# A dense DFT convolution and hand-made gelu replaced by a two-step FFT, row layernorms and one-instruction gelu

## The chip, the core and the metric

One core of a Trainium2 chip. The metric is the time of one execution on the device in microseconds (us), as a median over runs. Before: 714.38 us (713.78 to 715.79, 12 runs).

The engines are called PE (TensorE, matmul), PEld (its weight load, which overlaps PE), DVE (VectorE), ACT (ScalarE), POOL (GpSimd) and SP (SyncE, which issues most DMAs). PSUM is the memory that matmuls write, SBUF the main on-chip memory. Every engine carries out its own instructions in the order in which the built program has them, and waits for the others by semaphores. `L284` is line 284 of the kernel concerned.

## The reference, cut to what matters

`q`, `k`, `v` are [1, 2048, 512] in bf16, S = 2048, D = 512, F = 1792.

```python
def ln(x): return (x - mean(x)) / sqrt(var(x) + 1e-5)          # over the 512 channels
k_shift = sum(shift_k[:, 3 - t] * k_pad[:, t:t + S] for t in range(4))   # causal, 4 taps
kv = k_shift * v
y  = irfft(rfft(kv, 4096) * rfft(ssm_k, 4096))[:S] + kv * ssm_D        # along the sequence
h  = q + ln(q) * y
x  = ln(h)
g  = gelu(ln(x) @ w1)                                           # tanh form of gelu
hs = shift_four_channel_quarters(g, +1, -1, +2, -2) @ w2
x1 = x + hs
out = h + x1 + gelu(ln(x1) @ w3) @ w4
```

## The kernel before

It works channel by channel: a tile is [128 channels, 2048 positions], four of them. The long convolution is a dense Fourier transform by matmul. For each chunk of 128 frequencies, DVE and ACT generate a cosine and a sine table, and PE multiplies them into `kv` and the filter `hf`, 4 x 16 matmuls of 512 columns:

```python
for b in range(NB):                       # 16 blocks of 128 positions; 16 chunks around this loop
    nc.tensor.matmul(ghr[:], lhsT=lhs_c, rhs=hf[:, b, :], start=st, stop=sp)        # L258
    nc.tensor.matmul(akr[:], lhsT=lhs_c, rhs=kv_all[:, b, :], start=st, stop=sp)
    nc.tensor.matmul(ghi[:], lhsT=lhs_s, rhs=hf[:, b, :], start=st, stop=sp)
    nc.tensor.matmul(aki[:], lhsT=lhs_s, rhs=kv_all[:, b, :], start=st, stop=sp)
# ... copies to SBUF, complex product; then the inverse, 512 matmuls in the same manner (L319, L321)
```

Since a layernorm then runs across partitions, its sums are matmuls with a column of ones, and mean and scale are spread to all partitions by matmuls with diagonal matrices (`layernorm_feat`, L121 to L178). Gelu is six instructions, two on ACT and four on DVE:

```python
def gelu_psum(gp, psrc, dst):
    nc.scalar.copy(xs[:], psrc)
    nc.vector.tensor_tensor(out=u[:], in0=xs[:], in1=xs[:], op=MUL)
    nc.vector.tensor_scalar(out=u[:], in0=u[:], scalar1=GELU_C2, scalar2=GELU_C1, op0=MUL, op1=ADD)
    nc.vector.tensor_tensor(out=u[:], in0=u[:], in1=xs[:], op=MUL)
    nc.scalar.activation(sg[:], u[:], ACT.Sigmoid)
    nc.vector.tensor_tensor(out=dst, in0=xs[:], in1=sg[:], op=MUL)
```

## Time and profile before

| stage before | us | length | the busiest |
|---|---|---|---|
| loads, kv, layernorm of q, dense DFT and inverse | 0 to 460 | 460 | PE from 100 on |
| layernorm of h, w1, w2, layernorm of x1 | 460 to 577 | 117 | DVE |
| w3, gelu, w4, output | 577 to 713 | 136 | PE, held back by the gelu relay |

The first cut lies at the end of the inverse's last matmul, the second at the first MLP matmul. The lines of the profile behind this table are shown in the prediction. A window line there gives, for a stretch of time, what each engine was busy; a group line gives a kind of instruction with its count, total busy time, mean duration in ns, and the idle time of the engine before it with what ended it. The granted clock is the share of its full rate that PE was given.

### The profile page before, as it was taken

How to read it: one execution, taken by the hardware profiler on the slowest of the kernel's cores; microseconds unless marked ns; L12 is line 12 of the kernel's file. 1: busy time of each engine (PE TensorE's matmuls, PEld its weight loads, DVE VectorE, ACT ScalarE, POOL GpSimd, SP SyncE). 2: the span in 40 equal slices, each digit the busy share in tenths (PEclk: the TensorE clock that was granted, in tenths of full speed). 3: DMA queues.
4: the chain of work that ended last, by engine and by line, in shares of the span. 5: the costliest groups of instructions: out<-in, count | busy, mean ns of one | idle time of the engine just before them, and what ended most of it. 6: DMA issues, size and time to landing. Idle time of an engine off the chain costs nothing.

```text
span 712.8 us, 7378 instructions
## 1 busy us (share of the span) xinstructions
PE 544.7 (76%) x2800; PEld 244.9 (34%) x2800; DVE 526.8 (74%) x1000; ACT 339.2 (48%) x391; POOL 2.9 (0%) x11
## 2 busy tenths in 40 slices
PE   0122459999999999995799999833558468999976
PEld 0011324444444444442344444331223323433422
DVE  4699693756756766616989997179887788888974
ACT  0323317466466456512978787112470256445460
POOL 1000000000000000000000000000000000000000
PEclk9999999999999999998799999955699579999997
DMA  5646000000000000000000000080000000000000
GB/s 118 132 101 120 1 1 0 1 1 0 1 1 0 1 1 0 1 1 0 0 1 1 0 1 1 0 266 0 1 0 0 2 0 1 30 1 29 1 30 30
DMA packets 39925, 15.68 MB, mean 22 GB/s; under 512 B 34513, under 2 KB 39378, under 8 KB 39890
## 3 DMA queue, kind: packets, MB, share of 16 engines
q1 hardware_dynamic: 29234, 10.76, 6.2%
q10 hardware_dynamic: 10656, 4.46, 2.4%
q8 instruction: 22, 0.36, 0.2%
q14 instruction: 13, 0.11, 0.0%
HBM read 4.72 MB, written 2.10 MB: 10 GB/s over the span
## 4 chain that ended last, share of the span: by engine, by line
PE 57%; DVE 24%; ACT 11%; DMA 4%; issue 3%; SPq 0%; ACTq 0%; DVEq 0%
PE yps L319 8%; PE yps L321 8%; PE ghr L258 8%; PE ghi L260 8%; PE akr L259 8%; PE aki L261 8%; ACT xs L336 4%; DVE u L338 3%; PE po L412 3%; ACT sg L343 3%; DMA vT<-in_A_v_dram 2%; DVE tn L177 2%; DVE g_sb L344 2%; DVE u L339 2%; DVE ksh L210 2%
## 5 line engine op out<-in xcount | busy, mean ns | idle before, releaser
L319 PE MATMUL yps<-ics,Qr 128*128 128x512 bf16 x256 | 98.4, 384 | 12.1 <-ACT ics L113 12.1
L112 ACT ACTIVATE e<-t 128x2048 f32<-128x2048 f32 (+2 forms) x34 | 63.1, 1856 | 80.3 <-DVE t L110 79.9
L321 PE MATMUL yps<-iss,Qi 128*128 128x512 bf16 x256 | 98.3, 384 | 0.0
L258 PE MATMUL ghr<-hf,cs 128*128 128x512 bf16 x240 | 91.0, 379 | 0.0
L259 PE MATMUL akr<-kv_all,cs 128*128 128x512 bf16 x240 | 91.0, 379 | 0.0
L260 PE MATMUL ghi<-hf,ss 128*128 128x512 bf16 x240 | 91.0, 379 | 0.0
L261 PE MATMUL aki<-kv_all,ss 128*128 128x512 bf16 x240 | 91.0, 379 | 0.0
L107 DVE TENSOR_TENSOR e<-bj,rv 128x2048 f32<-128x2048 f32 (+2 forms) x34 | 75.7, 2226 | 16.7 <-ACT cs L113 11.8
L110 DVE TENSOR_TENSOR t<-e,t 128x2048 f32<-128x2048 f32 (+2 forms) x34 | 75.8, 2228 | 1.0
L412 PE MATMUL po<-g_sb,w_sb 128*128 128x512 bf16 x224 | 64.0, 392 | 10.5 <-DVE g_sb L344 6.8
L217 PE MATMUL pt<-ident,kvTc 128*128 128x128 bf16 x64 | 14.0, 274 | 61.7 <-DVE kvTc L214 29.2
L272 DVE TENSOR_TENSOR p<-acr,gcr 128x512 bf16<-128x512 bf16 x16 | 6.8, 426 | 71.4 <-ACT acr L266 56.4
L405 PE MATMUL pg<-ln1T,w_sb 128*128 128x512 bf16 x224 | 56.7, 385 | 3.6 <-ACT bbc L173 1.2
L343 ACT ACTIVATE sg<-u 128x512 bf16<-128x512 bf16 x72 | 45.3, 631 | 24.6 <-DVE u L341 23.0
L166 PE MATMUL psbc<-dga,ones_pp 128*128 128x128 bf16 x64 | 17.2, 269 | 44.8 <-DVE dga L163 44.8
L336 ACT CAST xs<-pg 128x512 bf16<-128x512 f32 x56 | 32.7, 584 | 36.0 <-DVE g_sb L344 21.0
L108 DVE TENSOR_SCALAR t<-e 128x2048 f32<-128x2048 f32 (+2 forms) x34 | 40.6, 1194 | 1.9
L113 ACT ACTIVATE ics<-e,halfpi 128x2048 bf16<-128x2048 f32 x16 | 32.1, 2004 | 20.8 <-PE yps L319 20.7
L338 DVE TENSOR_TENSOR u<-xs 128x512 bf16<-128x512 bf16 x72 | 30.5, 423 | 13.4 <-ACT xs L336 12.6
L321 PEld LDWEIGHTS <-Qi 128*128 128x128 bf16 x256 | 25.3, 99 | 42.4 <-DVE t L110 11.9
L319 PEld LDWEIGHTS <-Qr 128*128 128x128 bf16 x256 | 25.3, 99 | 32.6 <-issue 3.5
L412 PEld LDWEIGHTS <-w_sb 128*128 128x128 bf16 x224 | 21.3, 100 | 40.9 <-issue 24.8
(124 smaller groups left out, 838.3 us busy)
## 6 DMA issues: line engine op xcount, KB each, us to landing
out_dram<-osb SPq DMA_DIRECT2D x16, 128.0 KB, 1.8
w_sb<-in_B_w_dram SPq DMA_DIRECT2D x1, 1792.0 KB, 8.8
w_sb<-in_B_w_dram ACTq DMA_DIRECT2D x1, 1792.0 KB, 14.8
w_sb<-in_B_w_dram SPq DMA_DIRECT2D x1, 512.0 KB, 12.0
w_sb<-in_B_w_dram ACTq DMA_DIRECT2D x1, 512.0 KB, 15.8
hf<-in_A_ssm_k_dram SPq DMA_TRANSPOSE x16, 2.6
vT<-in_A_v_dram ACTq DMA_TRANSPOSE x4, 4.2
kT<-in_A_k_dram SPq DMA_TRANSPOSE x4, 4.1
```

The lines of the kernel that those rows point to most:

```text
L107: nc.vector.tensor_tensor(out=ev, in0=bj_b, in1=rv_b, op=MUL)
L110: nc.vector.tensor_tensor(out=tv, in0=ev, in1=tv, op=SUB)
L112: nc.scalar.activation(ev, tv, ACT.Abs)
L258: nc.tensor.matmul(ghr[:], lhsT=lhs_c, rhs=hf[:, b, :], start=st, stop=sp)
L259: nc.tensor.matmul(akr[:], lhsT=lhs_c, rhs=kv_all[:, b, :], start=st, stop=sp)
L260: nc.tensor.matmul(ghi[:], lhsT=lhs_s, rhs=hf[:, b, :], start=st, stop=sp)
L261: nc.tensor.matmul(aki[:], lhsT=lhs_s, rhs=kv_all[:, b, :], start=st, stop=sp)
L319: nc.tensor.matmul(yps[:, c, :], lhsT=Qr[:, q, c * P:(c + 1) * P], rhs=ics[:, qi, :], start=(q == 0), stop=False)
L321: nc.tensor.matmul(yps[:, c, :], lhsT=Qi[:, q, c * P:(c + 1) * P], rhs=iss[:, qi, :], start=False, stop=False)
L336: nc.scalar.copy(xs[:], psrc)
L343: nc.scalar.activation(sg[:], u[:], ACT.Sigmoid)
L412: nc.tensor.matmul(po[:], lhsT=w4_sb[:, k2, m * P:(m + 1) * P], rhs=g_sb[:, k2, :], start=(k2 == 0), stop=(k2 == FC - 1))
```

## The change

The intent is to take the arithmetic of the convolution from a dense DFT of about 1600 wide matmuls to some 250, by splitting 4096 points into 64 x 64; to keep positions on the partitions ("row layout"), where a layernorm is a DVE statistic over 512 neighbours; and to let ACT do gelu in one instruction straight out of PSUM. The price is an exchange of data between the two steps of the transform, which goes through scratch memory in DRAM: `zh_d`, `zk_d` and `v_d`, each 4.2 MB written and read back. The core of a diff that is 833 lines long:

```diff
-# dense: 16 chunks x 4 x 16 forward matmuls, 512 inverse ones, tables made for each chunk
+def step1(x, zd, b, zc):                      # first 64-point step, one block of rows
+    ps = ps_s.tile([P, 2, D], F32, name="ps1", tag="ps1")
+    for t in range(2):
+        nc.tensor.matmul(ps[:, t, :], lhsT=f1[:, t, :], rhs=x, start=True, stop=True)
+    evac(zc[:, :, b % 2, :], ps[:])           # copy to SBUF, ACT and DVE in turn ("AV")
+    if b % 2 == 1:
+        nc.sync.dma_start(zd[:].rearrange(...)[:, :, b - 1:b + 1, :], zc)    # to DRAM
... (shift filter: 16 matmuls of 128 columns a block with diagonal matrices, then)
+    nc.vector.tensor_tensor(out=xkv[:, b, :], in0=pk[:], in1=v_sb[:, b, :], op=MUL)
... (zh, zk read back transposed; per frequency k1 of 32, the second step)
+    nc.tensor.matmul(a[:], lhsT=la, rhs=zk[:, k1, :], start=True, stop=True)         # psa L284
+    nc.tensor.matmul(g[:, 0, :], lhsT=lr, rhs=zh[:, k1, :], start=True, stop=True)   # psg
+    nc.tensor.matmul(g[:, 1, :], lhsT=li, rhs=zh[:, k1, :], start=True, stop=True)
+    nc.scalar.copy(asb[:], a[:])
+    nc.vector.tensor_tensor(out=pr[:], in0=g[:], in1=asb[:]..., op=MUL)              # pr L290
... (two psv matmuls, a copy vst, a store to v_d; wv read back; then per block)
-layernorm_feat(...)                           # sums and broadcasts on PE
+nc.vector.bn_stats(st[:, i, :], h_sb[:, b, :])
+nc.vector.bn_aggr(mv[:, i, :], st[:, i, :])
+rstd(r1[:], mv[:, :, 1], 1.0, 1e-5)           # Newton root: 9 small DVE instructions
+nc.vector.tensor_scalar(out=hb[:], in0=h_sb[:, b, :], scalar1=mv[:, i, 0:1], scalar2=r2[:, i:i + 1],
+                        op0=SUB, op1=MUL)
-gelu_psum(gp2, pg[:], g_sb[:, k2, :])         # six instructions
+nc.scalar.activation(gs[:, f, :], pg[:], ACT.Gelu_apprx_tanh)
... (loads, tables, halo, output per block: cut)
```

## The prediction

> **What bounds the kernel now.** I read the page's engine totals first, then the windows cut at the places where the chain of waits changes engine, then the groups for durations. The page:
>
> ```profile
> span 712.8 us, 7378 instructions
> PE 544.7 (76%) x2800; PEld 244.9 (34%) x2800; DVE 526.8 (74%) x1000; ACT 339.2 (48%) x391; POOL 2.9 (0%) x11
> PE 57%; DVE 24%; ACT 11%; DMA 4%; issue 3%; SPq 0%; ACTq 0%; DVEq 0%
> ```
>
> The last line is the chain that ended last: TensorE (PE) carries over half of it, VectorE (DVE) a quarter. An average over five stages says little, so the windows (start:end, length, busy us of each engine with its count, granted clock, DMA share, GB/s):
>
> ```profile
> 0.00:100.00 100.00, 23.34 (x224) 13.13 (x225) 77.89 (x132) 29.39 (x52) 2.75 (x9) 1.00 0.41 84
> 100.00:334.00 234.00, 230.50 (x1056) 103.39 (x1056) 139.16 (x185) 117.54 (x115) 0.00 (x0) 1.00 0.00 1
> 334.00:460.00 126.00, 117.06 (x528) 51.39 (x527) 103.96 (x73) 90.39 (x48) 0.00 (x0) 0.95 0.00 1
> 460.00:577.00 117.00, 56.53 (x481) 29.45 (x482) 96.04 (x288) 36.46 (x64) 0.15 (x2) 0.70 0.12 41
> 577.00:712.80 135.80, 117.25 (x512) 47.54 (x510) 109.75 (x327) 65.46 (x113) 0.00 (x0) 0.95 0.05 16
> ```
>
> Five stages: loads, kv and one layernorm (100 us, DVE the busiest); the dense forward DFT (234 us, PE busy without a gap); the dense inverse DFT (126 us, PE again); layernorms, w1 and w2 (117 us, DVE 82% busy, PE half idle and its clock at 0.70); the MLP (136 us, PE paced by the hand-made gelu). The bound is therefore PE for 360 us and DVE, or the DVE-ACT relay, for the rest. The groups and the order of time give the unit costs:
>
> ```profile
> L258 PE MATMUL ghr<-hf,cs 128*128 128x512 bf16 x240 | 91.0, 379 | 0.0
> L405 PE MATMUL pg<-ln1T,w_sb 128*128 128x512 bf16 x224 | 56.7, 385 | 3.6 <-ACT bbc L173 1.2
> L415 DVE TENSOR_TENSOR tf<-po,x1T 128x512 f32<-128x512 f32 x16 | 10.7, 688 | 1.4 <-PE po L412 1.1
> L177 DVE TENSOR_TENSOR tn<-xT,abc 128x512 bf16<-128x512 bf16 x16 | 6.1, 420 | 1.4 <-ACT abc L172 1.4
> L268 ACT CAST gcr<-ghr 128x512 bf16<-128x512 f32 x16 | 9.3, 583 | 19.6 <-PE ghr L258 18.5
> L343 ACT ACTIVATE sg<-u 128x512 bf16<-128x512 bf16 x72 | 45.3, 631 | 24.6 <-DVE u L341 23.0
> ...
> 118.93 0.38 PE L258 MATMUL ghr<-hf,cs 128*128 128x512 bf16 x1
> 119.15 0.38 PE L259 MATMUL akr<-kv_all,cs 128*128 128x512 bf16 x1
> 119.36 0.38 PE L260 MATMUL ghi<-hf,ss 128*128 128x512 bf16 x1
> 119.30 0.60 ACT L268 CAST gcr<-ghr 128x512 bf16<-128x512 f32 x1
> 119.78 0.61 ACT L269 CAST gci<-ghi 128x512 bf16<-128x512 f32 x1
> ```
>
> What to see: a 512-wide matmul lasts 379 ns but the next starts 0.216 us after it, so its price is 0.216. An ACT copy of 512 lasts 0.60 and costs 0.48. DVE neighbours overlap too: in the chain of waits two L328 products reading PSUM (matmul memory) take 1.29 us and two bf16 L177 products 0.67, so 0.60 to 0.64 and 0.34 each. I sum with these start-to-start prices.
>
> **What the Trainium skill says.** (1) "TensorE: Matmul & The Clock Gate", section "Back-to-back issue gap": N/2.4 + 2.5 ns warm, 216 ns for 512 columns, and about 81 ns for a 128-wide matmul with its weight load. The trace agrees on 0.216; for 128-wide ones it has few free runs. (2) Same page, "What's actually happening": the PE clock halves when PE is idle enough and comes back with activity. The trace agrees: 0.70 in the layernorm stage, 1.00 in the dense DFT. (3) "VectorE: DVE Perf Modes", section "The perf-mode tier table": a tensor-tensor with a PSUM operand runs at one element per cycle, all-bf16 in SBUF at two. The trace agrees: 688 against 420 ns. (4) "DMA: Bandwidth & Descriptors", section "Anatomy of one DMA": about 2 us fixed per DMA, mostly the write receipt. The trace: 1.8 us for a 128 KB store. This matters because the change passes data through DRAM three times.
>
> **The change, part by part.** It is a rewrite. The dense DFT becomes a two-step FFT (64 x 64 points of 4096), the exchange between steps going through scratch DRAM (zh_d, zk_d, v_d, each 4.2 MB written and read back). Layernorms use rows, bn_stats and a DVE Newton root in place of PE sums, broadcast matmuls and a Sqrt table; gelu is one ACT instruction out of PSUM in place of two ACT and four DVE ones.
>
> PE, 512-wide matmuls. Removed: 1024 forward, 512 inverse, plus 48 for the Nyquist row: 1584 x 0.216 = 342 us. Added: 64 (step 1) + 96 + 64 (step 2 forward and inverse) + 32 (step 2 of the inverse, in stage_h) = 256 x 0.216 = 55 us. Kept: w1, w2, w3, w4 = 576 x 0.216 = 124 us. The 128-wide ones: 64 + 64 + 64 transposes, 256 for the shift filter by diagonal matrices, and 128 transposes later, about 576 x 0.08 = 46 us. So PE needs some 225 us in all. It can no longer be the bound throughout; I go by stages, by the order in which the built program has them.
>
> Stage 1, to the last zk write. Loads are 8.4 MB; the window 470 to 475 of the profile before moved 377 GB/s, so q lands near 27 us, ssm_k near 9. DVE waits in order for ssm_k (the dcol add stands second in its queue), so it starts near 9 us. Its work after that, in us: 16 PSUM copies of 1024 floats x 1.14 = 18; 8 bf16 copies of 1024 x 0.6 = 5; 16 kv products x 0.6 = 10; 8 table copies x 0.34 = 3; 16 bn_stats and bn_aggr x 0.7 = 11 (an estimate: one element per cycle, as the PSUM product); angles, Fourier tables, diag and small ones, about 11. Sum 58, so 67 at best. PE in the second half needs per pair of blocks 32 x 0.08 + 4 x 0.216 + 8 x 0.08 = 4.1 us, DVE also about 4.1: neither hides behind the other perfectly, and I take 80 us. Then zk's last write and the first read back, two DMAs one after the other: 3.5 us each (2 fixed, 1.5 for 0.5 MB). First step-2 matmul at 87 us.
>
> Stage 2, 32 frequencies: DVE 1024/0.96 + 0.07 = 1.14 us each, ACT 2 x 0.48 to 0.58 = 1.0 to 1.17, PE 5 x 0.216 = 1.08. All three are nearly equal, so I take 1.25 each: 40 us, with 3 for the first and last relay: 130. v_d's last write and wv's first read cannot begin sooner: 6 us. 136.
>
> Stage 3 first part (stage_h, w1, first w2). DVE for each of 16 blocks: 0.6 + 0.34 + 0.6 + 0.1 + 0.2 + 0.2 = 2.04, so 33; eight Newton roots of 9 small operations near 0.12 = 9; then until the first MLP matmul seven w2 results x 1.3 = 9, one root, the normalising and four residual sums: 3. Sum 54. PE has 124 x 0.216 + 80 x 0.08 = 33 there: hidden. With the relay DVE to PE to ACT to PE at group edges: 62. 198.
>
> Stage 3 second part. PE: 448 MLP matmuls + 32 of w2 = 480 x 0.216 = 104 us, 48 transposes 4, so 108. ACT gives a gelu per 0.6 us where PE needs 0.86: hidden. Waits for PSUM banks and for DVE at the first two groups' edges: 8. Last sum and store 3, clock not always full 3. 198 + 122 = 320.
>
> Summed against the stages before: 460 us of front and DFT become 136, 117 become 62, 136 become 122.
>
> **Rivals.** (a) DMA bounds stage 1. From 9 to 80 us it moves about 6.3 + 4.2 + 4.2 + 4.2 = 19 MB: 267 GB/s. For it: the case's best is 377, seen for loads alone, never for stores of 2 KB pieces. If stores run at half that, stage 1 takes some 25 us more: 345. Against: each piece is 1 or 2 KB, not the small pieces of the transposing loads before. (b) PE's half clock. If the 128-wide matmuls and transposes do not wake the clock, stage 1's pairs cost 8 us, not 4 to 5, and stage_h becomes PE-bound: +35 us, 355. For it: clock 0.50 in the window 470 to 475, full of tiny matmuls. Against: 0.90 in the stretch 505 to 536 before, with PE half busy by matmuls 512 wide. (c) Perfect overlap: stage 1 at 70, stage 2 at 39, part one of stage 3 at 56 and no bank waits: 290. (d) The exchange eats the gain: it would need 390 us more than I count; nothing in the profile speaks for it.
>
> **Range and chances.** The centre is 320. Half of (a) or (b) gives 332 to 338; both 380, unlikely. (c) gives 290. I take 290 to 352. A change within 2% would need 380 us that no sum here shows: faster 0.99, same 0.005, slower 0.005.
>
> **What would show it right or wrong.** In the profile after: first step-2 product near 87 us; its 32 products 1.2 to 1.3 us apart, DVE over 85% busy; a hole of about 6 us in PE at 130; stage_h with DVE over 80% busy; from about 200 us PE over 90% busy at clock 1.0 to the end. It is wrong if the DMA share is near 1.0 through stage 1 (rival a), if the clock shows 0.5 in stage 1 or stage_h (rival b), if ACT and not DVE is the releaser of the step-2 matmuls, or if the MLP part lasts well over 122 us.

## The result, and the profile after

The changed kernel takes 299.74 us (median of 9 runs, 299.24 to 303.78; the run of 303.78 was slow and is left out of the ratio). The ratio is 0.4199, 95% interval 0.4188 to 0.4211. Ratios here are the mean time of one kernel's fast runs over that of the other's in the same rounds, so not quite the ratio of the medians quoted.

The page of the kernel after, its totals and its chain of waits, which answer to the first fence of the prediction:

```profile
span 298.1 us, 3878 instructions
PE 238.8 (80%) x1410; PEld 119.4 (40%) x1410; DVE 190.3 (64%) x452; ACT 129.8 (44%) x205; POOL 14.5 (5%) x39
PE 50%; DVE 25%; DMA 14%; ACT 7%; issue 2%; SPq 1%; POOL 0%; DVEq 0%; ACTq 0%
```

PE has half its matmuls left, DVE less than half its instructions. DMA on the chain grew from 4% to 14%. Some 14 us of that, 5%, are the two exchanges shown below; another 16 us is a stretch of stage 2 where the chain passes through two stores of `v_d` while the engines work on beside them. (The DMA share of the chain also holds the first load of `ssm_k`, 6.5 us, and a store of `zk`, 5.3.) Next, the windows after, cut at the hand-over points between stages (start:end, length, busy us of PE, PEld, DVE, ACT and POOL with their counts, granted clock, DMA share, GB/s):

```profile
10.20:70.90 60.70, 48.14 (x514) 34.29 (x514) 58.47 (x102) 33.53 (x35) 8.75 (x18) 1.00 0.79 298
70.90:77.50 6.60, 1.04 (x4) 0.41 (x5) 3.87 (x12) 0.00 (x0) 0.00 (x0) 0.72 0.57 199
77.50:121.60 44.10, 40.46 (x156) 15.31 (x155) 37.98 (x32) 34.48 (x64) 0.18 (x2) 0.93 0.82 274
121.60:128.80 7.20, 1.38 (x4) 0.56 (x5) 0.31 (x1) 0.00 (x0) 0.00 (x0) 0.74 0.62 215
128.80:190.70 61.90, 44.09 (x222) 20.86 (x221) 57.71 (x211) 21.07 (x37) 1.66 (x4) 0.78 0.13 48
190.70:298.10 107.40, 103.58 (x512) 47.85 (x511) 31.22 (x90) 39.44 (x68) 0.00 (x0) 1.00 0.06 20
```

Six stretches: stage 1 (DVE busy 58.5 of 60.7 us, PE 48); a hole in which PE does 1 us of work; the 32 frequencies of stage 2 (PE 40, DVE 38, ACT 34 of 44); a second hole; stage_h with w1 and the first w2 blocks (DVE 57.7 of 61.9); and the MLP, where PE is busy 103.6 of 107.4 us at full clock. The holes are in the chain of waits in order of time (start, us, what):

```profile
70.95 2.73 DMA zk_d<-zc
73.77 3.72 DMA zk<-zk_d
77.53 0.60 PE psa L284
...
121.53 2.14 DMA v_d<-vst
124.83 5.28 DMA wv<-v_d
...
246.08 12.09 PE pg L442 x56
258.17 12.09 PE po L452 x56
```

Each hole is a store and a load, one after the other: 2.73 + 3.72, then 2.14 + 5.28 with about 1 us of issuing between. No compute engine's work lies between them. The last two lines show a part of the MLP: 56 matmuls in 12.09 us, 0.216 each, nothing between them. The groups with the unit costs:

```profile
L444 ACT ACTIVATE gbuf<-pg 128x512 bf16<-128x512 f32 x56 | 33.5, 598 | 38.4 <-PE pg L442 38.3
L442 PE MATMUL pg<-lnT,w_sb 128*128 128x512 bf16 x224 | 49.3, 379 | 0.3 <-ACT lnT L183 0.3
L290 DVE TENSOR_TENSOR pr<-psg,asb 128x1024 bf16<-128x1024 f32 x32 | 38.0, 1223 | 7.5 <-ACT asb L288 4.9
L288 ACT CAST asb<-psa 128x512 bf16<-128x512 f32 x32 | 18.9, 593 | 9.5 <-PE psa L284 8.1
```

ACT's gelu (L444) takes 598 ns, as much as a plain copy (593), and waits 38.4 us for PE: it paces nothing. PE in turn waits 0.3 us in the whole MLP. The price of the shift filter's 128-wide matmuls comes from a line of PE's timeline in stage 1 (start, us, instructions merged):

```profile
53.00 1.73 PE L228 MATMUL pk<-diag,kT 128*128 128x128 bf16 x28
```

The stages side by side:

| stage | before | after | saved | predicted after |
|---|---|---|---|---|
| up to the inverse's result in SBUF | 460 | 128.8 | 331 | 136 |
| residual, layernorms, w1, w2 up to the first MLP matmul | 117 | 61.9 | 55 | 62 |
| MLP and output | 136 | 107.4 | 29 | 122 |
| span | 712.8 | 298.1 | 415 | 320 |

(The last two terms of `h` lie in the first row before and in the second row after; by the prediction's prices they are 16 x (0.6 + 0.34) = 15 us of DVE.)

Inside the first row: the first step-2 matmul began at 77.5 (predicted 87), stage 2 took 44.1 (43), the second hole 7.2 (6). By the first step-2 matmul I mean `psa`, L284, which needs `zk`; four `psg` ones, which do not, ran at 71 us already. Below, the kv loop is the second half of stage 1, which makes `xkv` and its first transform step two blocks at a time (a pair).

### The profile page after: what moved, and what is told of

The parts are those of the page before. It is cut to its first block, busy times and chain, and to the rows that moved or that the text cites. A ratio compares the mean times of both kernels' runs of the same rounds, so it can differ in the third digit from the quotient of the medians.

```text
span 298.1 us, 3878 instructions
## 1 busy us (share of the span) xinstructions
PE 238.8 (80%) x1410; PEld 119.4 (40%) x1410; DVE 190.3 (64%) x452; ACT 129.8 (44%) x205; POOL 14.5 (5%) x39
## 4 chain that ended last, share of the span: by engine, by line
PE 50%; DVE 25%; DMA 14%; ACT 7%; issue 2%; SPq 1%; POOL 0%; DVEq 0%; ACTq 0%
PE pg L442 16%; PE po L452 16%; DMA v_d<-vst 6%; PE pw L395 4%; DVE st L378 3%; PE ps L196 3%; DVE zc L185 3%; DMA zk_d<-zc 3%; DVE ty L376 2%; DMA hnat<-in_A_ssm_k_dram 2%; PE ptx L362 2%; ACT zch L183 2%; DVE pr L290 2%; DMA wv<-v_d 2%; PE psa L284 2%
## 5 line engine op out<-in xcount | busy, mean ns | idle before, releaser
L444 ACT ACTIVATE gbuf<-pg 128x512 bf16<-128x512 f32 x56 | 33.5, 598 | 38.4 <-PE pg L442 38.3
L442 PE MATMUL pg<-lnT,w_sb 128*128 128x512 bf16 x224 | 49.3, 379 | 0.3 <-ACT lnT L183 0.3
L452 PE MATMUL po<-w_sb,gbuf 128*128 128x512 bf16 x224 | 49.3, 379 | 0.0
L455 DVE TENSOR_TENSOR ob<-po,qn 128x512 bf16<-128x512 f32 x16 | 11.0, 690 | 57.7 <-PE po L452 57.7
L290 DVE TENSOR_TENSOR pr<-psg,asb 128x1024 bf16<-128x1024 f32 x32 | 38.0, 1223 | 7.5 <-ACT asb L288 4.9
L452 PEld LDWEIGHTS <-gbuf 128*128 128x128 bf16 x224 | 21.8, 98 | 25.9
L288 ACT CAST asb<-psa 128x512 bf16<-128x512 f32 x32 | 18.9, 593 | 9.5 <-PE psa L284 8.1
L301 ACT CAST vst<-psv 128x512 bf16<-128x512 f32 x32 | 18.8, 587 | 7.4 <-PE psv L298 5.1
L395 PE MATMUL pw<-hnT,w 128*128 128x512 bf16 x64 | 19.1, 460 | 1.4 <-ACT hnT L183 1.4
L228 PE MATMUL pk<-diag,kT 128*128 128x128 bf16 x256 | 16.9, 219 | 0.2 <-POOL kT L221 0.2
L228 PEld LDWEIGHTS <-kT 128*128 128x128 bf16 x256 | 15.5, 98 | 3.6 <-POOL kT L221 0.3
```

The costliest lines, as they stand in the source:

```text
L228: nc.tensor.matmul(pk[:, c * P:(c + 1) * P], lhsT=kT[:, c, 3 + b - j, :], rhs=diag[:, c, j, :], start=(j == 0), stop=(j == 3))
L288: nc.scalar.copy(asb[:], a[:])
L290: nc.vector.tensor_tensor(out=pr[:], in0=g[:], in1=asb[:].unsqueeze(1).to_broadcast([P, 2, D]), op=MUL)
L301: nc.scalar.copy(vst[0][:, k1 % 2, :], ps[:])
L395: nc.tensor.matmul(pw_[:], lhsT=w1_sb[:, k, m * P:(m + 1) * P], rhs=hnT[:, k, g * 512:(g + 1) * 512], start=(k == 0), stop=(k == DC - 1))
L442: nc.tensor.matmul(pg[:], lhsT=w3_sb[:, k, f * P:(f + 1) * P], rhs=lnT[:, k, g * 512:(g + 1) * 512], start=(k == 0), stop=(k == DC - 1))
```

## The experiments

My theory: the gain is the DFT's matmuls first, gelu second, and inside stage 1 the sum of DVE's work is the bound. Rivals: gelu costs nothing once DVE is free elsewhere; stage 1 is bound by DMA or by the relay between engines. Twelve kernels ran, each with 3 or 5 rounds against the kernel before. No run separates the FFT from the row layout, because neither part stands alone in this kernel. The edits are cut to their core; further lines that follow from them are left out.

**1. The gelu alone, in the kernel before (`b_gelu`).**

```diff
-        (the six instructions of gelu_psum)
+        nc.scalar.activation(dst, psrc, ACT.Gelu_apprx_tanh)
```

> The kernel before with one part of the change alone: its six-instruction gelu replaced by one ACT gelu out of PSUM. Theory 1 (the hand-made gelu paces the w1 and MLP stages of the kernel before): the MLP stage goes from 136 us to what PE needs, 448 x 0.216 = 97, plus 64 transposes and four group edges, some 108; the w1 stage from 27 to about 16. Sum -39, so 675 us. Theory 2 (PE and its clock pace those stages and gelu is hidden): less than -10, so over 704.

680.94 us (678.52 to 682.24), ratio 0.9525 (0.9499 to 0.9552): 34 us less. The w1 matmuls went from 27.3 to 16.4 us, the MLP from 136.0 to 113.7. The group of the gelu in this kernel:

```profile
L335 ACT ACTIVATE g_sb<-pg 128x512 bf16<-128x512 f32 x56 | 33.3, 597 | 57.9 <-PE pg L396 57.9
```

One instruction of 597 ns now waits for PE instead of PE waiting for a relay of six. The Trainium skill, page "ScalarE: Activation LUTs", section "What ACT_TABLE_LOAD costs", gives an ACTIVATE with immediate operands 186 ns + 0.833 ns per element, whatever the function, so by estimate 612 for 512; the 597 measured are 15 less. The theory's 675 was 6 us too low, nearly all of it in the MLP (113.7 for an expected 108): this kernel still has its output transposes on PE and a clock of 0.95 there.

**2. The gelu taken back out of the kernel after (`a_oldgelu`).** Both calls of the one-instruction gelu get the six-instruction body again.

> The changed kernel with the six-instruction gelu put back. Theory 1 (DVE, which gets 1.22 us per tile more, becomes the bound wherever gelu runs): +20 us in the DVE-bound front part (16 tiles) and +20 in the MLP part (17 us per group of 14 tiles where PE needs 12.1), so about 340. Theory 2 (DVE is only 29% busy in the MLP part and hides it there): about 320.

339.57 us (337.55 to 341.16), ratio 0.4751 (0.4729 to 0.4772): 40 us more, as the theory said, but divided otherwise: the first MLP matmul starts 12 us later (202.7) and the MLP takes 132.6 us in place of 107.4, so 12 and 25 where the theory had 20 and 20. Its window of the MLP's last 107 us:

```profile
228.00:335.00 107.00, 92.63 (x420) 38.36 (x417) 84.68 (x234) 56.16 (x98) 0.00 (x0) 1.00 0.06 20
```

PE does 420 matmuls in the same 107 us in which the kernel after did 512, because the relay (DVE 84.7, ACT 56.2 busy) paces it. So gelu is worth 34 us in one kernel and 40 in the other, and the other 375 to 381 us belong to the FFT and the row layout together.

**3. More copies on ACT (`a_evac`).** By the windows, DVE was full in stage 1 and ACT half idle, so this should have shortened it.

```diff
-    def evac(o, i, pat="AV"):
+    def evac(o, i, pat="AAV"):
```

> The changed kernel with two of three PSUM copies of stage 1 on ACT, not one of two: 64 copies, so about 11 leave DVE, some 9 us of its 58. Theory 1 (DVE bounds stage 1): the first step-2 matmul, at 77.5 us, comes 6 to 8 us sooner, and the whole takes 292 to 294. Theory 2 (the DMA traffic, or the relay between engines, bounds stage 1): no change, or slower because ACT gets the longer copies: 299 to 302.

309.48 us (307.69 to 310.53), ratio 0.4334 (0.4324 to 0.4343): 10 us slower, with DVE's busy total down from 190.3 to 184.0. Neither expectation held. The first step-2 matmul came at 84.9 in place of 77.5. DVE's timeline of this run (start, us, instruction; in brackets the idle time before it and what ended it):

```profile
48.89 1.06 DVE L325 TENSOR_SCALAR qn<-q_sb,qmv,qrs 128x512 bf16<-128x512 bf16 x3 [3.34 <-POOL qrs L256]
```

The built order had changed with the durations: `qn` stands ahead of the kv products in DVE's queue, and waits 3.34 us for a root that POOL computes in one slow instruction. The products behind it wait too. A second reason is in the pattern: a cycle of three falls in step with the pairs of the loops, so ACT got all eight `xh` copies (1.03 us there) and six of the eight `kT` copies, which lengthened the relay PE to ACT to PE early on. No run tells how the 7 us by which the step-2 matmul came later divide between the two.

**4. The same idea without the pattern (`a_evac2`).** The `xh` and `kT` copies stay on DVE, the table copies go to ACT, and of step 1's copies two in three.

> The changed kernel with the short bf16 copies that PE waits for next (xh, kT) all on DVE, where one takes 0.68 us and not 1.02, the table copies all on ACT, and two of three of the float copies zch and zc on ACT. DVE's sum falls by about 4 us only. Theory 1 (sum of DVE work): the first step-2 matmul comes 3 to 4 us sooner, total near 296. Theory 2 (relay latency): more than that, since each xh and kT step is 0.34 us shorter on half of 16 steps, but zc on ACT is not on its path: total 293 to 296. If, as in the first run that moved copies, the built order makes DVE wait for something late, it is slower than 300; then the order is what counts, not the sums.

304.68 us (303.56 to 305.54), ratio 0.4269 (0.4255 to 0.4283): 5 us slower. The first step-2 matmul came at 82.0, 4.5 us later. Again a `qn` waits for POOL in the kv loop (2.76 us), and PE was busy for only 7.5 us between 60 and 70 us, where it had 9.0 in the kernel after; the rest of the 4.5 us I did not trace. Two runs in which DVE had less to do were slower. Since both changed the order as well, they only suggest that the sum of DVE's work is not what sets stage 1; run 5 tests it.

**5. Less DVE work, copies as they were (`a_nostat`).** Twelve of the sixteen statistics of `q` are left out. It is wrong, though the result stayed within the tolerance.

```diff
-    for b in range(NB):
+    for b in range(4):
         nc.vector.bn_stats(qst[:, b, :], q_sb[:, b, :])
         nc.vector.bn_aggr(qmv[:, b, :], qst[:, b, :])
```

> The changed kernel, with a result that is wrong on purpose: 12 of the 16 row statistics of q (bn_stats and bn_aggr, about 0.68 us a pair) are left out of stage 1 and the first four are used again. No copy changes its engine, so nothing in the relay between PE, ACT and DVE gets longer, unlike in the run that moved copies to ACT and was slower. Theory 1 (the sum of DVE work bounds stage 1): the first step-2 matmul, at 77.5 us, comes about 8 us sooner, total near 292. Theory 2 (the relay PE to copy to PE with two buffers, or the DMA traffic, bounds it, and the statistics only fill DVE's gaps): it moves by less than 3 us.

300.5 us (298.78 to 301.38), ratio 0.4205 (0.4189 to 0.4222): the same. The first step-2 matmul stood at 77.6, against 77.5. The kv loop of the kernel after, on DVE:

```profile
50.04 1.21 DVE L185 CAST zc<-ps 128x1024 bf16<-128x1024 f32 x1
51.16 1.28 DVE L230 TENSOR_TENSOR xkv<-pk,v_sb 128x512 bf16<-128x512 f32 x2
52.36 0.42 DVE L185 COPY tt<-pt 128x512 bf16<-128x512 bf16 x1
52.69 0.18 DVE L254 BATCH_NORM_AGGREGATE qmv<-qst 128x2 f32<-128x6 f32 x1
52.78 0.67 DVE L253 BATCH_NORM_STATS2 qst<-q_sb 128x6 f32<-128x512 bf16 x1
53.36 1.21 DVE L185 CAST zc<-ps 128x1024 bf16<-128x1024 f32 x1
```

One pair of blocks every 3.32 us, DVE not idle in these lines. And without the statistics:

```profile
53.71 1.23 DVE L185 CAST zc<-ps 128x1024 bf16<-128x1024 f32 x1 [0.76 <-PE ps L196]
54.85 1.28 DVE L230 TENSOR_TENSOR xkv<-pk,v_sb 128x512 bf16<-128x512 f32 x2
56.94 1.22 DVE L185 CAST zc<-ps 128x1024 bf16<-128x1024 f32 x1 [0.81 <-PE ps L196]
```

Still one pair every 3.23 us. Where the statistics stood, DVE now waits for PE's step-1 matmul. The windows from 60 to 70 us, first of the kernel after:

```profile
60.00:70.00 10.00, 9.03 (x116) 6.69 (x113) 9.79 (x17) 4.55 (x5) 2.86 (x1) 1.00 0.51 195
```

and of the run without the statistics:

```profile
60.00:70.00 10.00, 9.39 (x126) 7.46 (x125) 8.26 (x12) 4.62 (x7) 0.00 (x0) 1.00 0.67 241
```

PE is 90% busy in the first and 94% in the second. The statistics filled time that DVE would have spent waiting: 96% busy was no proof of a bound. Not all of the 8 us left stage 1, though. The root on POOL, now for 4 columns, took 1.04 us and not 2.93, and the built order moved the sixteen `qn`, twelve of which had stood in the hole after stage 1, to between 33 and 47 us: DVE's busy time up to 70.9 us fell by 3.9 only (54.6 for 58.5), and the first kv product came 1.0 us later (45.1). The loop itself, from the first to the last kv product, took 23.9 us in place of 24.9.

**6. Less work on PE too (`a_pknostat`).** As run 5, and the shift filter with two of its four taps, so half of its matmuls. It is wrong as well.

```diff
-            for j in range(4):
+            for j in range(2):
                 nc.tensor.matmul(pk[:, c * P:(c + 1) * P], lhsT=kT[:, c, 3 + b - j, :], rhs=diag[:, c, j, :],
-                                 start=(j == 0), stop=(j == 3))
+                                 start=(j == 0), stop=(j == 1))
```

> The changed kernel, wrong on purpose: 12 of 16 row statistics of q left out, as in the run before that moved nothing, and with it half of the 256 small shift-filter matmuls (two taps of four; 128 x 0.057 = 7 us of PE). Theory 1 (in the kv loop of stage 1 DVE and PE are each near 3.2 us per pair of blocks, so that taking from one alone shows nothing): with both lightened the loop falls to the DMA or relay pace, the first step-2 matmul comes 3 to 7 us sooner than 77.5, total 293 to 297. Theory 2 (the loop is paced by the relay kv product, step-1 matmuls, copy, whatever the loads are): no change, 299 to 301.

298.26 us (297.49 to 299.39), ratio 0.4169 (0.4160 to 0.4179): 1.5 to 2 us less. The kv products ended 2.6 us sooner, a pair every 2.8 us, but the first step-2 matmul only came at 76.6, 0.9 us sooner. Its chain of waits says why:

```profile
62.44 6.22 DMA zk_d<-zc
68.78 1.24 DVE zc L185
70.07 2.73 DMA zk_d<-zc
```

With DVE and PE both relieved, a store is next in line: the last copy waits for a buffer whose store took 6.22 us, where the same DMA takes a median of 3.5 in the kernel after. The wait is not new: the chain of the kernel after also passes through one `zk` store, of 5.27 us, at 54.6, after which DVE stood idle for 0.47. I read from runs 5 to 7 that DVE, PE and DMA are close to each other in the kv loop, and that relieving one moves the wait to the next; no run took DMA away.

**7. More DMA (`a_dma2`).** Each store of `zk` is issued a second time, into an unused scratch area: 4.2 MB more in stage 1.

```diff
             nc.sync.dma_start(zd[:].rearrange("(t p) b d -> p t b d", p=P)[:, :, b - 1:b + 1, :], zc)
+            if zd is zk_d:
+                nc.sync.dma_start(zx_d[:].rearrange("(t p) b d -> p t b d", p=P)[:, :, b - 1:b + 1, :], zc)
```

> The changed kernel with every zk store issued twice, the second time into scratch that nobody reads: 4.2 MB more DMA traffic between 45 and 72 us, on top of about 8 MB there. Theory 1 (DVE or the relay bounds stage 1 and DMA has slack): first step-2 matmul 0 to 3 us later, total 300 to 303. Theory 2 (rival (a) of the prediction, DMA bounds stage 1): 4.2 MB at the 0.4 MB per us of the busiest slices is 10 us more: 310.

306.08 us (304.08 to 307.61), ratio 0.4285 (0.4266 to 0.4304); the first step-2 matmul at 83.7, 6.2 us later, between the two expectations. Its window from 60 to 70 us:

```profile
60.00:70.00 10.00, 8.47 (x111) 6.90 (x113) 9.74 (x18) 3.13 (x5) 1.39 (x1) 1.00 1.01 360
```

The DMA share is 1.01 at 360 GB/s where the kernel after has 0.51 at 195, and in the profile ACT waits 6.4 us for buffers held by the extra stores, one of which stands in the chain of waits with 6.50 us. Alone, the stores leave some room; 4.2 MB more are too many.

**8. Half of DVE's product in stage 2 (`a_half`).** `pr` is computed for 256 of the 512 columns, the rest stays zero. It is wrong.

```diff
-        nc.vector.tensor_tensor(out=pr[:], in0=g[:], in1=asb[:].unsqueeze(1).to_broadcast([P, 2, D]), op=MUL)
+        nc.vector.tensor_tensor(out=pr[:, :, 0:H], in0=g[:, :, 0:H], in1=asb[:, 0:H].unsqueeze(1).to_broadcast([P, 2, H]), op=MUL)
```

> The changed kernel, with a result that is wrong on purpose: the product of step 2 is made for half of the columns only, so DVE needs about 0.6 us per frequency and not 1.2; PE and ACT do all they did. Theory 1 (DVE, ACT and PE are nearly equal in stage 2): the 44.1 us of the stage fall to what ACT needs, 32 x 1.1 and the ends, 40 to 42, total 296 to 298. Theory 2 (DVE alone is the bound and the others have room): under 38 us. Theory 3 (the v_d stores and the weight loads hold the copies up): no change.

298.51 us (297.48 to 299.73), ratio 0.4181 (0.4165 to 0.4197): its interval overlaps that of the kernel after. Its window of stage 2:

```profile
78.80:122.00 43.20, 38.02 (x152) 14.78 (x155) 20.80 (x32) 34.49 (x64) 0.17 (x2) 0.94 0.84 285
```

DVE's busy time fell from 38.0 to 20.8 us and the stage from 44.1 to 41.5 (its last `vst` copy ended at 120.4). PE and ACT hold it almost as tightly as DVE did. This was the theory's reading (40 to 42 us): three nearly equal engines. PE and ACT were not lightened in any run, and stores have a part too: the chain of waits passes through `v_d` stores for 16.1 us in the kernel after and 9.3 here (see run 11).

**9. Fewer small instructions in stage_h (`a_root`).** `stage_h` computes two roots, r1 and r2, one after the other. Here both go through one set of instructions of width 8, and every root has one Newton step in place of two, which leaves 52 small DVE instructions of 108. The result is correct.

```diff
-        rstd(r1[:], mv[:, :, 1], 1.0, 1e-5)
-        rstd(r2[:], mv[:, :, 1], 1.0 + 1e-5, 1e-10)
+        rstd2(r12[:], mv[:, :, 1])            # r1 = r12[:, 0:4], r2 = r12[:, 4:8]
```

> The changed kernel with fewer small DVE operations in the layernorm roots: the two roots of a group in one set of instructions eight columns wide, and one Newton step, not two (7 instructions per group and not 18; 6 and not 9 for the later root). Theory 1 (DVE bounds the stretch from 129 to 191 us): about 50 instructions of some 0.085 us leave it there, so -4 us: 296. Theory 2 (the relay DVE to PE to ACT, or the half clock of PE, bounds it): within 1 us of 300.

297.26 us (296.13 to 297.37), ratio 0.4156 (0.4146 to 0.4167), an interval that does not touch that of the kernel after. From the first `py` matmul to the first MLP matmul it took 58.6 us in place of 63.3, with DVE's busy total down by 4.3. Here DVE's work does set the pace: taking instructions away shortened the stage by as much. It is not all: PE's clock has a share, as said below under rival (b).

**10. The table transposes later (`a_tt`).** The 64 transposes of the tables for the inverse stand in the middle of the kv loop. They are queued behind the last step-1 matmul.

```diff
-                nc.tensor.transpose(pt[:, j, :], src, ident[:])
+                with tc.issue_after(last_mm.ins):
+                    nc.tensor.transpose(pt[:, j, :], src, ident[:])
```

> The changed kernel, correct, with the 64 table transposes (0.057 us each on PE, 16 copies after them) queued behind the last step-1 matmul: out of the kv loop, into the 6.6 us in which PE waits for zk's store and first load. Theory 1 (the kv loop is bound by PE and DVE together): per pair PE loses 0.46 of 3.1 us and DVE 0.33, so the loop of 8 pairs is 2 to 4 us shorter and the transposes cost nothing in the hole: 296 to 298. Theory 2 (relay pace or DMA): no gain, or a loss of 1 to 2 us where the transposes or their copies hold up the first step-2 product: 300 to 302.

306.46 us (305.13 to 306.74), ratio 0.4280 (0.4271 to 0.4288): 6 to 7 us slower, so neither expectation held. DVE's timeline:

```profile
58.09 0.41 DVE L327 TENSOR_SCALAR qn<-q_sb,qmv,qrs 128x512 bf16<-128x512 bf16 x1 [3.34 <-POOL qrs L258]
```

The slot freed on DVE was refilled with `qn`, which waits for POOL as in run 3. And the transposes cost 9 us in their new place (75 to 84 us), not the 4 expected, because each group of four needs its copy before the buffer comes free. The first step-2 matmul came at 84.1.

**11. The w3 and w4 loads later (`a_wlate`).** They are queued behind the reads of `wv`, so that they do not share the DMA engines with the stores of `v_d`.

```diff
-        nc.sync.dma_start(w3_sb[:], B_w3.rearrange("(k p) o -> p k o", p=P))   # after the last zk read
+    with tc.issue_after(wv_last.ins):
+        nc.sync.dma_start(w3_sb[:], B_w3.rearrange("(k p) o -> p k o", p=P))   # w4 likewise
```

> The changed kernel, correct, with the loads of w3 and w4 (3.6 MB) taken out of stage 2 and queued behind the reads of wv. In the profile ACT waits twice for v_d stores in stage 2, 1.5 us in all. Theory 1 (those loads delay the stores): -1 to -2 us. Theory 2 (the stores are late by themselves, and the loads now delay wv's later reads and the layernorm stage): 0 to +2.

300.26 us (298.79 to 300.68), ratio 0.4192 (0.4182 to 0.4203): inconclusive. In its profile ACT no longer waits for `v_d` (1.5 us in the kernel after) and all later stages come 1.4 to 1.5 us sooner, but the time cannot be told from 0.4199; the profile is that of its fastest run (298.79).

**12. Runs 9 and 11 together (`a_best`).**

> The two small gains together: the roots r1 and r2 in one set of instructions with one Newton step, and the w3 and w4 loads queued behind the reads of the inverse. Theory: the first shortened stage_h and w1 by 4.7 us and the whole by 3, the second let the inverse's results be stored and read back 1.5 us sooner; they lie one after the other, so they add up to 4 to 4.5 us: about 295.5 us, ratio near 0.414, first MLP matmul near 185. Rival: the later loads gained nothing that lasts (their own run gave 0.4192 against 0.4199), because DVE, not the read, sets the pace after the exchange: then 297, ratio 0.4156 as with the roots alone.

295.16 us (294.12 to 297.72, 5 runs), ratio 0.4138 (0.4123 to 0.4152); the first MLP matmul at 184.5. It is the fastest kernel here, 1.5% under the kernel after. That the later loads add to the gain of run 9 is likely but not shown: the two intervals overlap (0.4146 to 0.4167 there).

## Why the prediction was right

The time predicted was 320 (290 to 352), and it became 299.74. The mechanism held, stage by stage; two terms of the sum were too large, one unit price was too high and one too low.

- **The bound before and what is removed.** Right. The stages that held the dense DFT are those that lost the most, 331 us of 415; 360 of their 460 us were the DFT and its inverse, with PE busy for 348. Run 1 and run 2 put gelu at 34 and 40 us.
- **Stage 1: "I take 80 us".** Mis-sized by 9. The sum of DVE's work was right (58 predicted, 58.47 busy), and its start near 9 to 10 as well; but of the 13 us of padding for imperfect hiding only 4 came, for the last `zk` store left at 70.9. Half of the reason given for the padding was a wrong price: a 128-wide matmul was taken at 0.08 us. In the kernel after, 28 of the filter's matmuls run in 1.73 us, of which 0.22 is the last one's own duration: 0.056 each. At that price PE needs, per pair of blocks, 32 x 0.056 + 4 x 0.216 + 8 x 0.056 = 3.1 us, not 4.1; the loop was measured at 3.3. That the sum of DVE's work predicts the stage was partly luck: run 5 shows that in the kv loop the statistics only fill gaps.
- **The exchange: "3.5 us each".** Right in sum for the first: 2.73 + 3.72 in the chain, for 7, and 7.2 for the second hole where 6 was predicted.
- **Stage 2: "All three are nearly equal, so I take 1.25 each".** Right, 44.1 for 43, with DVE 86% busy and the products 1.30 us apart. Run 8 supports the equality. What the sum left out is the stores: without w3 and w4 beside them (run 11), ACT's 1.5 us of waiting for `v_d` are gone.
- **Stage 3, first part: 62.** Right at 61.9, with terms that cancel. A normalising `tensor_scalar` (hb, hn) costs 0.32 from start to start, not 0.2: 408 ns long, in place of the 291 of the immediate form. The 32 of them in stage_h alone are 32 x 0.12 = 4 us more. Also nine w2 results, not seven, were done before the first MLP matmul. DVE's sum became 57.7 for 54, and of the 8 for group edges 4 came. Run 9 shows that DVE's work does set the pace of this stage.
- **Stage 3, second part: 122.** Mis-sized by 15, the largest miss. PE's own work was 4 too high, 108 for 103.8 (its last matmul ended at 294.5): only 16 w2 matmuls were left for this part, not 32, since 48 stood before it. (The prediction's 28 and 32 are also 4 short of the 64 that there are.) The "8" for PSUM banks and edges and the "3" for the clock did not occur: PE waits 0.3 us and the clock is 1.00. The tail did: the last sum takes 0.69 and its store the rest of 3.6, for the "3". That six PSUM buffers and gelu's 0.6 us against PE's 0.86 leave no edge to pay is my reading; no run changed the buffers.
- **Rival (a), DMA bounds stage 1.** Not as put: the DMA share over stage 1 was 0.79, not near 1. But DMA is close behind: a store is in the chain of waits already, run 6 met another, and 4.2 MB more cost 6.2 us in run 7.
- **Rival (b), half clock.** Wrong for stage 1 (1.00), half right for stage_h (0.78 in the window, 0.60 from 141 to 151 us and 0.57 from 166 to 174). It cost far less than the 35 us feared, but something: the chain of waits passes through two runs of 14 w1 matmuls of 5.10 and 5.57 us, 0.36 and 0.40 each in place of 0.216, so by estimate 4.6 us more than at full rate. DVE stood idle behind them for 1.12 and 1.48 us. No run changed the clock alone.
- **Rival (c), perfect overlap at 290.** Nearest in stage 1 (70 for 70.9) and in the MLP; not in stages 2 and 3a, where its 39 and 56 were 44 and 62.

What stays open: how much of the first row's 331 us belongs to the FFT and how much to row statistics in place of PE sums, and why stage 1's loop would not go below 2.8 us per pair even with half the filter; the store of 6.22 us in run 6 suggests DMA, but no run took DMA away.

## What to carry to other kernels

Sum each engine's work per stage at start-to-start prices, and trust the sum where one engine stands clear of the others; pad it little for waits that no line shows (of the 13, 8 and 11 us put in here, some 4, 4 and 0 came). Where two or three engines are close to each other, as in the kv loop, a busy share of 96% did not prove a bound: take the work away and see what ends the wait next. And before moving work between engines, look at what the built order will then put at the head of each queue: three "relieving" edits made this kernel 5 to 10 us slower, each time with DVE waiting 2.8 to 3.3 us for one slow POOL instruction ahead of other work in its queue.

## What the Trainium skill lacked or had wrong

- "TensorE: Matmul & The Clock Gate", section "Back-to-back issue gap", gives sustained rates of about 81 ns for 128 columns and 131 for 512, each with its weight load, and says that its formula for a lone matmul is too high for 512. Here the formula was right in both cases: 0.056 us in streams of 28 matmuls of 128 columns with new weights each (1.73 us in all), 0.216 for 512 (56 in 12.09 us). Elsewhere the same page gives back-to-back rates of 55.6 and 215.7 ns, which agree. Using 81 ns cost the prediction part of its miss in stage 1.
- "VectorE: DVE Perf Modes", section "The perf-mode tier table", has one row for `tensor_scalar`. With two per-partition operands on bf16 [128 x 512] it took 408 ns here, with two immediates 291.
- The same table has no row for batch statistics. `bn_stats` on bf16 [128 x 512] took 667 to 686 ns, 0.60 from start to start, which is the rate of a product out of PSUM; `bn_aggr` took 168 to 176 ns.
- No page that I found prices a power on GpSimd: [128 x 16] float32 took 2.93 us, and DVE waited 2.8 to 3.3 us for it in three runs.
- "DMA: Bandwidth & Descriptors", section "Anatomy of one DMA — SWDGE (gpsimd) path", fits 2.0 us plus the bytes at 436 GB/s to a DMA issued from GpSimd. I found no such fit for one issued from SP, as all are in the kernel after. There a store of 128 KB took 1.8 us in all (median) and one of 512 KB 3.2 to 3.5. Nor did I find a price for an exchange through DRAM inside a kernel: a store followed by the dependent load left PE with 1.0 us of work in 6.6, and with 1.4 in 7.2.
